# Seven block products instead of eight in the spatial product of batches 2 to 7

## Chip, core and metric

One core of one Trainium2 chip. The metric is device time in microseconds, the median of several executions; the kernel before takes 1388.6 us (1387.6 to 1389.8 in four runs). TensorE is written PE, VectorE DVE, ScalarE ACT, GpSimd POOL, SyncE SP, as in the profile.

## The reference

```python
X = np.fft.fft(np.fft.fft(x, axis=1), axis=2).real   # x: 8 x 3072 x 256
h = np.maximum(X @ w_in, 0.0)                        # d_ff = 1024
u, v = h[..., :512], h[..., 512:]
v_n = (v - mean(v)) / sqrt(var(v) + 1e-6)            # over the last axis
v_s = einsum('ts,bsd->btd', w_spatial, v_n) + b_spatial[None, :, None]
out = (u * v_s) @ w_out                              # 8 x 3072 x 256, fp32
```

The product with `w_spatial` (3072 x 3072, called W) is most of the work. `w_spatial` is drawn with a standard deviation of 0.01/3072 and the bias is 1, so the product adds some 0.01/3072 x sqrt(3072) = 0.0002 to a 1. This matters for reading the runs: the comparison with the reference hardly sees W (one experiment below uses wrong operands of W and passes). "Correct" says that nothing else was broken; that the sums are right rests on the code.

## The kernel before

The Fourier transform is done as folds on DVE followed by small cosine products on PE ("prep" of the next batch, spread over the current one in numbered steps). W is turned and cast to bf16 during batch 0 and kept in DRAM as 24 tiles of 128 x 6 x 512 (768 KB). Each batch streams them through a ring of five:

```python
def load_wt(c, g):
    wt = wtpool.tile([P, GK, TC], BF16, name="wt", tag="wt")       # ring of 5
    nc.sync.dma_start(out=wt, in_=wtd[c][g])
    return wt

def spatial(v, wt, pw, g, dt):                # 4 PSUM banks, one for each dt
    for kk in range(GK):
        k = GK * g + kk
        nc.tensor.matmul(pw, lhsT=v[:, k, 128 * dt:128 * dt + 128], rhs=wt[:, kk, :],
                         start=(k == 0), stop=(k == KT - 1))

def gate(c, pw, ut):
    gt = gpool.tile([P, TC], BF16, name="gt", tag="gt")
    tm = tpool.tile([P, TC], FP32, name="tm", tag="tm")
    nc.vector.tensor_tensor(out=tm, in0=pw, in1=bbc[:, TC * c:TC * c + TC], op=ALU.add)
    nc.vector.scalar_tensor_tensor(out=gt, in0=ut, scalar=0.0, in1=tm, op0=ALU.max, op1=ALU.mult)
    return gt
# ... (cut)
# one step of the main loop: 6 matmuls, then whatever prep is due at this step
for dt in range(NDT):
    spatial(cur.v, wts[ti], pws[dt], g, dt)
    if g == NG - 1:
        gts.append(gate(c, pws[dt], uts.pop((c, dt))))
    # ... (cut: turning of W, projection, u)
    for f in steps[4 * (NG * ci + g) + dt]:
        f()                                  # folds, transforms, v of the next batch
```

## Time and profile before

| | us |
|---|---|
| median time | 1388.6 |
| start until the first spatial product | 71 |
| batch 0 (with the turning of W) | 212 |
| batches 1 to 6, each | 158.4 |
| batch 7 (no prep beside it) | 151 |

The lengths are worked out from the trace: from the first weight load of a batch's spatial product to that of the next. The lines of the profile are shown in the prediction below.

### The profile page before, as it was taken

The page shows a single profiled execution, that of the slowest core. Times are in us where ns is not written, and L with a number is a line of the kernel's source. Part 1 is how long each engine was busy: PE and PEld are TensorE (multiplying, and loading weights), DVE is VectorE, ACT ScalarE, POOL GpSimd, SP SyncE. Part 2 cuts the span into 40 slices and gives each one's busy share as a digit, 9 for nine tenths or more (in the row PEclk, how much of TensorE's full clock was granted, in tenths as well). Part 3 has the DMA queues.
Part 4 walks back from the last instruction along what each step waited for, and adds up shares of the span by engine and source line. Part 5 has one row for each costly group of instructions (what it writes and reads, how often), then busy time and mean ns, then how long its engine had stood idle before and what let it go on. Part 6 is the DMA issues. An engine that isn't in the chain of part 4 may idle for free.

```text
span 1384.1 us, 18120 instructions
## 1 busy us (share of the span) xinstructions
PE 1321.3 (95%) x6967; PEld 651.3 (47%) x6967; DVE 842.1 (61%) x1694; ACT 516.9 (37%) x890; POOL 128.6 (9%) x167
## 2 busy tenths in 40 slices
PE   1768999999999999999999999999999999999998
PEld 0434455544444444444444444444444444444444
DVE  7656657775567747675557746776466746762323
ACT  7863146521444134531444224530445214441110
POOL 8355134410000000000000000000000000000000
PEclk9989999999999999999999999999999999999999
DMA  7899699785444543356344653456344553444441
GB/s 241 290 361 336 201 296 301 277 313 176 156 134 150 197 171 130 137 185 226 107 137 150 201 168 130 132 182 227 107 139 148 178 185 111 136 154 160 150 147 54
DMA packets 105254, 255.28 MB, mean 184 GB/s; under 512 B 17584, under 2 KB 64336, under 8 KB 105168
## 3 DMA queue, kind: packets, MB, share of 16 engines
q1 hardware_dynamic: 65840, 196.66, 42.3%
q10 hardware_dynamic: 29824, 44.05, 8.8%
q0 software_dynamic: 9504, 13.42, 3.1%
q8 instruction: 54, 0.88, 0.3%
q14 instruction: 32, 0.26, 0.1%
HBM read 210.80 MB, written 56.62 MB: 193 GB/s over the span
## 4 chain that ended last, share of the span: by engine, by line
PE 87%; DMA 5%; DVE 3%; ACT 2%; POOL 2%; issue 1%; ACTq 0%; SPq 0%; POOLq 0%; DVEq 0%
PE pw L624 68%; PE po L640 6%; DMA wr<-in_moe_w_spatial_dram 3%; PE pu L602 3%; PE pv L526 2%; PE pe L461 1%; PE pud L604 1%; PE pd L553 1%; PE pt L204 1%; DVE tm L630 1%; DMA xr<-in_x_dram 1%; DVE gt L631 1%; DMA wtd<-wx 1%; POOL xr L129 1%; POOL wb L191 0%
## 5 line engine op out<-in xcount | busy, mean ns | idle before, releaser
L624 PE MATMUL pw<-wt,v_t 128*128 128x512 bf16 x4512 | 1025.2, 380 | 7.8 <-ACT v_t L588 6.3
L624 PEld LDWEIGHTS <-v_t 128*128 128x128 bf16 x4608 | 446.4, 98 | 528.0 <-issue 10.8
L644 ACT COPY ot<-po 128x512 f32<-128x512 f32 x96 | 56.3, 586 | 403.6 <-PE po L640 392.2
L630 DVE TENSOR_TENSOR tm<-pw,bbc 128x512 f32<-128x512 f32 x192 | 131.5, 685 | 100.4 <-PE pw L624 90.3
L588 ACT ACTIVATE v_t<-r,rs 128x512 bf16<-128x512 f32 x96 | 78.4, 817 | 89.0 <-DVE rs L586 82.7
L640 PE MATMUL po<-wob,gt 128*128 128x256 bf16 x768 | 99.7, 273 | 1.7 <-DVE gt L631 1.7
L607 ACT ACTIVATE up<-pu 128x512 bf16<-128x512 f32 x96 | 57.3, 597 | 113.0 <-PE pu L602 73.6
L191 POOL CAST wb<-wr 128x768 bf16<-128x768 f32 x87 | 77.2, 893 | 134.8 <-PE pt L204 91.3
L640 PEld LDWEIGHTS <-gt 128*128 128x128 bf16 x768 | 74.7, 98 | 29.8 <-DVE gt L631 2.2
L574 DVE BATCH_NORM_STATS2 stt<-r 128x6 f32<-128x512 f32 x108 | 72.5, 680 | 23.6 <-ACT r L567 22.0
L204 PE MATMUL pt<-ident,wb 128*128 128x128 bf16 x576 | 48.9, 228 | 29.8 <-POOL ident L275 21.7
L580 ACT ACTIVATE rs<-mv,epst 128x2 f32<-128x2 f32 x96 | 28.5, 297 | 124.3 <-DVE mv L576 115.0
L631 DVE SCALAR_TENSOR_TENSOR gt<-up,tm 128x512 bf16<-128x512 bf16 x96 | 69.2, 720 | 3.3
L631 DVE SCALAR_TENSOR_TENSOR gt<-um,tm 128x512 bf16<-128x512 bf16 x96 | 67.2, 700 | 3.3
L204 PEld LDWEIGHTS <-wb 128*128 128x128 bf16 x576 | 41.0, 102 | 50.4 <-ACT wb L189 24.4
L567 ACT ACTIVATE r<-r 128x512 f32<-128x512 f32 x84 | 52.8, 628 | 28.2 <-DVE r L561 26.5
L526 PE MATMUL pv<-weo,eo_t 128*128 128x512 bf16 x192 | 57.8, 382 | 3.4 <-ACT r L536 2.7
L554 ACT ACTIVATE r<-pv 128x512 f32<-128x512 f32 x84 | 49.3, 587 | 27.0 <-PE pv L526 26.7
L602 PE MATMUL pu<-eo_t,weo 128*128 128x512 bf16 x192 | 57.5, 381 | 0.0
L562 DVE BATCH_NORM_STATS2 stt<-r 128x6 f32<-128x512 f32 x84 | 57.4, 684 | 0.0
L590 DVE TENSOR_SCALAR v_t<-r,mv,rs 128x512 bf16<-128x512 f32 x96 | 52.4, 546 | 0.0
L209 ACT COPY wt<-pt 128x768 bf16<-128x768 bf16 x44 | 35.1, 797 | 33.4 <-PE pt L204 33.3
(599 smaller groups left out, 1008.3 us busy)
## 6 DMA issues: line engine op xcount, KB each, us to landing
wt<-wtd SPq DMA_DIRECT2D x168, 768.0 KB, 4.4
wr<-in_moe_w_spatial_dram SPq DMA_DIRECT2D x69, 384.0 KB, 3.7
out_dram<-ot ACTq DMA_DIRECT2D x88, 256.0 KB, 3.9
wtd<-wt ACTq DMA_DIRECT2D x20, 768.0 KB, 5.3
xr<-in_x_dram POOLq DMA_DIRECT2D x32, 384.0 KB, 13.6
xt<-in_x_dram SPq DMA_DIRECT2D x21, 512.0 KB, 4.0
xt<-xr SPq DMA_DIRECT2D x21, 512.0 KB, 5.0
wr<-in_moe_w_spatial_dram SPq DMA_DIRECT2D x23, 383.5 KB, 7.0
```

What stands on the lines that cost most here:

```text
L191: nc.gpsimd.tensor_copy(out=wbs[i], in_=src)
L204: nc.tensor.transpose(pt[:, kk, :], wb[:, 128 * kk:128 * kk + 128], ident)
L526: nc.tensor.matmul(pv, lhsT=eo[:, kt, sl], rhs=weo[:, kt, DH:], start=(kt == 0), stop=(kt == 1))
L562: nc.vector.bn_stats(out=stt[:, 0, :], in_=r[0])
L574: nc.vector.bn_stats(out=stt[:, n, :], in_=r[n])
L588: nc.scalar.activation(out=v[:, k, :], in_=r[0], func=AF.Identity, scale=rs[:, 0:1], bias=rs[:, 2:3])
L602: nc.tensor.matmul(ps, lhsT=weo[:, kt, wd], rhs=eo[:, kt, sl], start=(kt == 0), stop=(kt == 1))
L607: nc.scalar.activation(out=up, in_=ps, func=AF.Relu)
L624: nc.tensor.matmul(pw, lhsT=v[:, k, 128 * dt:128 * dt + 128], rhs=wt[:, kk, :], start=(k == 0), stop=(k == KT - 1))
L630: nc.vector.tensor_tensor(out=tm, in0=pw, in1=bbc[:, TC * c:TC * c + TC], op=ALU.add)
L631: nc.vector.scalar_tensor_tensor(out=gt, in0=ut, scalar=0.0, in1=tm, op0=ALU.max, op1=ALU.mult)
L640: nc.tensor.matmul(po[:, i, :], lhsT=gts[dt][:, t0:t0 + 128], rhs=wob[:, dt, :], start=(dt == 0), stop=(dt == NDT - 1))
```

## The change

Split W into 2 x 2 blocks of 1536 and V into 2 x 2 blocks of 1536 x 256; the product takes seven products of sums of blocks (Winograd's form of Strassen's method) instead of eight. The sums of W do not depend on the batch: they are made once, beside batch 1, from the tiles that pass through, and stored in DRAM. The sums of V are made in every batch. Intent: 72 of 576 matmuls fewer in each of six batches.

```diff
+    class Sums:                                   # beside batch 1
+        def pool(self, k):                        # 18 times, 128 x 3072 bf16
+            o, x_, y_ = {1: (y22, y21, y22), 3: (y21, x11, y21), 4: (y21, x12, y22)}[k]
+            nc.gpsimd.tensor_tensor(out=o, in0=x_, in1=y_, op=ALU.add if k == 1 else ALU.subtract)
+        def two(self, n):                         # 12 halves on DVE
+            nc.vector.tensor_tensor(out=y22[:, sl], in0=y22[:, sl], in1=x11[:, sl], op=ALU.subtract)
+        def store(self, k):
+            nc.sync.dma_start(out=std[k - 1][c][h], in_=y22 if k < 3 else y21)
 ... (cut)
+    def t_sum(v, k, h):                           # sums of V, 8 a batch, 128 x 1536 bf16
+        e = nc.gpsimd if k in (4, 1) else nc.vector
+        e.tensor_tensor(out=o, in0=x_, in1=y_, op=ALU.add if k == 2 else ALU.subtract)
 ... (cut)
+    def after(p, d, pw, bt, bb, us):              # eviction of product p
+        a0, a1, a2 = (acc(k, d) for k in range(3))
+        if p == 1:
+            nc.scalar.copy(out=a1, in_=pw)
+            nc.gpsimd.tensor_tensor(out=a2, in0=a1, in1=bt, op=ALU.add)
+        elif p == 6:
+            plus(a1, pw, a1)                      # DVE, one input in PSUM
+            nc.gpsimd.tensor_tensor(out=a0, in0=a1, in1=bt, op=ALU.add)
+            nc.gpsimd.tensor_tensor(out=a1, in0=a1, in1=bb, op=ALU.add)
+        elif p == 7:
+            plus(a1, pw, a1)
 ... (cut: products 4, 2, 5, 3 with the gates)
+            for pi, p in enumerate(ORDP):         # [1, 6, 7, 4, 2, 5, 3], for each of 3 pairs of chunks
+                pws = [psW.tile([P, TC], FP32, name="pw", tag="psW") for _ in range(2)]
+                for h in range(2):
+                    wt = fetched[at]              # ring of 5, 42 tiles a batch instead of 24
+                    for d in range(2):
+                        for j in range(GK):
+                            nc.tensor.matmul(pws[d], lhsT=station(p, cur.v, h, j, d),
+                                             rhs=wt[:, j, :], ...)
```

Besides: bias is loaded per chunk instead of once, x is loaded from ACT's queue instead of SP's, some normalisations move from DVE to ACT, and the folds are cut into six parts at steps of their own (`FOLD2`).

## The prediction

> **What bounds the kernel now.** I read the page's engine shares and slices first, then the chain that ended last, then the groups of instructions, then the windows by stage, and last the waits of TensorE and the timeline of VectorE where GpSimd works beside it.
>
> ```profile
> PE 1321.3 (95%) x6967; PEld 651.3 (47%) x6967; DVE 842.1 (61%) x1694; ACT 516.9 (37%) x890; POOL 128.6 (9%) x167
> PE   1768999999999999999999999999999999999998
> POOL 8355134410000000000000000000000000000000
> DMA  7899699785444543356344653456344553444441
> PE 87%; DMA 5%; DVE 3%; ACT 2%; POOL 2%; issue 1%; ACTq 0%; SPq 0%; POOLq 0%; DVEq 0%
> ```
>
> TensorE is busy without a gap from slice 4 on and holds 87% of the chain that ended last; the DMA is half idle there, and GpSimd has nothing to do after slice 9. The chain's lines give 68% to L624, the spatial product. By stage (columns: stretch, length, busy time of PE, PEld, DVE, ACT, POOL, clock, DMA share, GB/s):
>
> ```profile
> 80.00:100.00 20.00, 16.48 (x114) 8.79 (x113) 11.34 (x32) 11.83 (x21) 6.71 (x9) 0.89 1.03 390
> 120.00:281.00 161.00, 157.12 (x1009) 84.41 (x1008) 114.36 (x217) 70.62 (x118) 58.40 (x69) 1.00 0.80 277
> 597.00:754.00 157.00, 157.00 (x792) 75.92 (x790) 100.05 (x205) 56.59 (x101) 0.00 (x0) 1.00 0.47 159
> ```
>
> One steady batch fills TensorE wholly, VectorE to 64%, ScalarE to 36%, and moves 159 GB/s. Busy time of a pipelined matmul is not its cost, so I take the cost from the chain in order of time (start, length, what):
>
> ```profile
> 751.57 11.65 PE pw L624 x54
> 910.23 11.65 PE pw L624 x54
> ```
>
> 54 spatial matmuls take 11.65 us, 0.2158 us each. The same place of two successive batches is 158.66 us apart (910.23 - 751.57; other places give 158.4), of which 576 x 0.2158 = 124.3 us are the spatial product. The other 34 us (projection, u, v, transforms) the change leaves alone. Groups that I use below:
>
> ```profile
> L624 PE MATMUL pw<-wt,v_t 128*128 128x512 bf16 x4512 | 1025.2, 380 | 7.8 <-ACT v_t L588 6.3
> L630 DVE TENSOR_TENSOR tm<-pw,bbc 128x512 f32<-128x512 f32 x192 | 131.5, 685 | 100.4 <-PE pw L624 90.3
> L631 DVE SCALAR_TENSOR_TENSOR gt<-up,tm 128x512 bf16<-128x512 bf16 x96 | 69.2, 720 | 3.3
> L588 ACT ACTIVATE v_t<-r,rs 128x512 bf16<-128x512 f32 x96 | 78.4, 817 | 89.0 <-DVE rs L586 82.7
> L590 DVE TENSOR_SCALAR v_t<-r,mv,rs 128x512 bf16<-128x512 f32 x96 | 52.4, 546 | 0.0
> ```
>
> L624 waited 7.8 us in the whole run: nothing but the count of matmuls can shorten the steady stages.
>
> **What the Trainium skill says.** (1) "VectorE: DVE Perf Modes", the section on the TRN2 errata, gives 215 ns for a 512-wide matmul and 691 ns for a 512-wide fp32 add; the trace has 215.8 and 685, so both costs are at their floor. (2) "GPSIMD Engine Reference", section 3.1, puts a two-input elementwise operation at about 2.6 cycles an element at 1.2 GHz. The trace has one such warm operation, 128x258 in 696 ns (L332), against 559 by the rule, so about 0.14 us of start more. Estimates from it: 512 wide 1.25 us, 1536 wide 3.5, 3072 wide 6.8. (3) "SBUF — State Buffer", "Who interferes with whom": a VectorE instruction with two SBUF inputs, or in a 2-port mode, contends with GpSimd. The trace agrees; the first line is beside GpSimd's casts, the second without them:
>
> ```profile
> 126.00 0.68 DVE L361 COPY ef<-sm 128x8 f32<-128x8 f32 x1
> 144.98 0.17 DVE L361 COPY ef<-sm 128x8 f32<-128x8 f32 x1
> ```
>
> (4) "HBM Reference", "Specifications (TRN2)": a core streaming alone gets about 425 GB/s. The best 20 us here moved 390.
>
> **The change, part by part.** *Removed:* for batches 2 to 7 the 2x2 block product takes 7 products instead of 8. Each is 3 chunks x 2 x 2 x 6 = 72 matmuls, so 504 stand for 576: 72 x 0.2158 = 15.54 us a batch, all on the path, and six batches give **-93.2 us**.
>
> *VectorE, a steady batch:* for each of three pairs of chunks there are now 14 adds from PSUM and 8 gate multiplies where there were 8 and 8, so 42 + 24 a batch stand for 24 + 24: 18 x 0.685 = +12.3. Four sums of V (1536 wide; at the fold's fp32 rate of 1.23 us for 1024 at most 1.8 each): +7. Moved to ScalarE: 12 normalisations x 0.546 = -6.6 and four evictions of the transform (L508, 1.07) = -4.3. Net about +8: 108 of 143 us, 76% instead of 64%. ScalarE gets 6 copies (0.59), 12 normalisations (0.82), 4 evictions (1.12, as L463): +18, so 74 of 143. GpSimd gets 18 adds of 1.25 and 4 sums of 3.5: 36.5 us. None reaches 143, so by busy time all of it lies beside TensorE. What matters is lateness: a product has two PSUM banks of four, and its banks must be evicted within the next product, 24 matmuls or 5.2 us, plus what else stands in between. With VectorE at 76% and in order, some products will be late. I choose 1.7 us a batch: **+10**.
>
> *DMA, a steady batch:* 42 operand tiles of 0.786 MB for 24, plus 1.6 MB of bias: 25.0 MB (159 GB/s x 157 us) become 40.7, or 285 GB/s over 143 us. Today 159 GB/s cost a share of 0.47, so the new share is about 0.84. Hidden, if the ring of five tiles evens out the bursts.
>
> *Batch 1:* GpSimd forms 18 sums of 3072: 18 x 6.8 = 122 us of 158, in a tight order: a ring slot is freed only when the sums using it have been stored. Each of the three rounds has GpSimd operations back to back, four steps (6.6 us) apart, exactly their estimated length; beside them VectorE has about 56 us of instructions that share its port (3 folds x 6.9, 24 gates x 0.7, 12 normalisations x 0.55, 12 half sums near 1). Slack before a tile comes late I work out as 5 us a round: 46 us at the fifth sum's planned end, 4.4 for a store, 4.4 for the load, against the use at 59. I take 3 us lost a round: **+9**. At the seam to batch 2 the last sums, their stores and five loads follow each other with no work beside: **+4**.
>
> *Start:* the 1.5 MB bias load leaves the stretch where the DMA share is above 1: **-1** (up to 4).
>
> Sum: 1389.5 - 93.2 + 10 + 9 + 4 - 1 = **1318 us**, 5.1% faster.
>
> **The rivals.** *Loads become the bound.* In the first chunk of a batch fall 14 tiles (11.0 MB), three x loads (3.15), the turning of x (1.6), the outputs of two chunks (1.05) and bias (0.5): 17.3 MB in 42 us (168 x 0.2158 + u 2.6 + projection 3.5), 409 GB/s. Four tiles in hand make it (17.3 - 3.1) / 42 = 338. The 390 GB/s of the start speaks against a stall, the 277 at share 0.80 and the x bursts on another queue for one. If 300 GB/s is all there is, 5 us a batch are lost: about 1335 to 1345.
>
> *VectorE and GpSimd block each other.* If GpSimd's 36 us hold VectorE for half of that, VectorE is at 88% and the products wait 5 us a batch: some 1338. The stretched copy above speaks for it; against it, that most added adds read PSUM and one SBUF input.
>
> *Batch 1 is bound by GpSimd.* If 122 us and the 56 us of VectorE exclude each other, the batch takes 178 us or more instead of 158: +20 to +40 in place of my +9, 1330 to 1350.
>
> **Range and chances.** All waits gone gives 1389.5 - 93.2 - 4 = 1292, below the range since tight orders seldom run free. One rival in full gives about 1345, the upper end. Only two or three in full bring less than 2% (above 1362). So 1299 to 1345, faster 0.92, same 0.06, slower 0.02.
>
> **What would show it.** Right: the page after has 432 fewer spatial matmuls; batches 3 to 6 lie 143 to 146 us apart; TensorE's waits there are on VectorE's adds and sum to under 3 us a batch; batch 1 lasts 160 to 170 us; DMA share near 0.84. Wrong: a distance above 148 with waits on the operand tile (loads) or on the adds (VectorE); GpSimd's 3072-wide sum far from 6.8 us; batch 1 above 175; a first batch that is longer because its chunks wait for bias.

## More of the kernel before

A batch has three folds. Each reads one x tile of 1 MB (`xt`, a single buffer) and loads the next only when it is done with it. A fold is fourteen short DVE instructions, of which twelve read two SBUF tensors and two copy a few elements.

## The result

1425.1 us (1422.7 to 1425.5), against 1388.6: ratio 1.026 (95% interval 1.024 to 1.028), 2.6% slower. A ratio here is the mean time of one kernel's runs over that of the other's of the same rounds, so not quite the ratio of the medians quoted. Executions over 1.5% slower than the fastest of the same kernel are left out of the means. The page after: engine shares, slices and the chain by engine.

```profile
PE 1267.4 (89%) x6535; PEld 619.2 (44%) x6535; DVE 1022.5 (72%) x1759; ACT 588.3 (41%) x1006; POOL 452.2 (32%) x317
```

```profile
PE   1779999978879777999879989999799989999998
POOL 8354134162454552221420250123220152025210
PEclk9989999988989898999999999999999999999999
DMA  7799689725737397779767897689767877778985
```

```profile
PE 67%; DVE 18%; DMA 9%; issue 3%; ACT 2%; POOL 1%; ACTq 0%; SPq 0%; DVEq 0%; POOLq 0%
```

The 432 matmuls are gone (6967 - 6535). But PE now has gaps from slice 8 on where it had none, DVE has 18% of the chain instead of 3%, and the granted clock dips after the start too (mean 0.959; 0.995 before). By batch:

| us | start | b0 | b1 | b2 | b3 | b4 | b5 | b6 | b7 |
|---|---|---|---|---|---|---|---|---|---|
| before | 70.8 | 211.6 | 158.4 | 158.4 | 158.4 | 158.7 | 158.4 | 158.4 | 151.0 |
| after | 71.4 | 212.5 | 217.7 | 162.3 | 158.6 | 152.3 | 158.4 | 153.3 | 136.7 |

By arithmetic batches 2 to 6 should take 158.4 - 15.5 = 142.9. So 59 us were lost in batch 1, 70 in batches 2 to 6 (784.9 against 5 x 142.9 = 714.5), and about 1 us in each of the others. The stage view, for batch 1 before, then for batches 1 and 3 after (stretch, length, busy time of PE, PEld, DVE, ACT, POOL, clock, DMA share, GB/s):

```profile
283.00:441.50 158.50, 158.50 (x798) 76.60 (x797) 101.33 (x207) 56.72 (x102) 1.43 (x2) 1.00 0.52 178
283.80:501.50 217.70, 174.29 (x797) 80.09 (x796) 178.32 (x215) 56.37 (x102) 103.89 (x17) 0.89 0.51 188
663.90:822.50 158.60, 147.02 (x726) 70.71 (x725) 118.61 (x213) 70.19 (x124) 38.98 (x26) 0.97 0.78 269
```

In batch 1 DVE is busy for 178 us with about as many instructions as it did in 101 us before. The timelines say why. First GpSimd's, then DVE's, then PE's, in batch 1 (start, length, what, and in brackets the idle time before it and its releaser):

```profile
303.88 6.85 POOL L912 TENSOR_TENSOR wt<-zone,wt 128x3072 bf16<-128x3072 bf16 x1
310.69 5.98 POOL L912 TENSOR_TENSOR wt<-wt 128x3072 bf16<-128x3072 bf16 x1
316.74 6.30 POOL L912 TENSOR_TENSOR wt<-zone,wt 128x3072 bf16<-128x3072 bf16 x1
```

```profile
304.91 5.85 DVE L399 COPY ef<-sm 128x8 f32<-128x8 f32 x1
310.79 6.42 DVE L401 TENSOR_TENSOR ef<-sm 128x508 f32<-128x508 f32 x1
317.24 6.08 DVE L408 TENSOR_TENSOR od<-ef 128x258 bf16<-128x258 f32 x1
323.25 0.41 DVE L409 TENSOR_TENSOR evf<-ef 128x258 f32<-128x258 f32 x1
```

```profile
306.88 2.75 PE L678 MATMUL pw<-wt,v_t 128*128 128x512 bf16 x12
324.85 7.69 PE L678 MATMUL pw<-zone,v_t 128*128 128x512 bf16 x24 [15.22 <-DVE tm L694]
```

A copy of eight elements, 0.17 us undisturbed, takes 5.85. DVE and GpSimd alternate: each GpSimd sum holds one DVE instruction for its whole length, and as soon as that has run the next sum holds the next one. DVE works in order, so the gate (`tm`, L694) behind the fold starts at 324.11, though the first matmuls that it evicts had ended at about 305, and PE waits 15.2 us for the PSUM banks. An instruction that reads PSUM and one SBUF tensor (L694) kept its 0.68 us throughout (0.66 to 0.72 in all 192). PE's waits for these gates in batch 1:

```profile
PE pw L678 <- DVE tm L694: 36.4, 8, 15.2
```

The idle PE then loses its clock. "TensorE: Matmul & The Clock Gate", Part 1, says that it falls to half after an idle window of about 3.4 us; the trace agrees: the clock records of batch 1 hold 48 us at half clock, in multiples of 3.4 us, and before there were none after the start. At a mean of 0.89 this is at most 24 of the 59 us, part of it while PE idled anyway; PE's waits in batch 1 sum to 43 us, which leaves about 16 for it.

In a steady batch both kinds of trouble appear, here at batch 3 (DVE with one line of GpSimd, PE, then ACT's queue):

```profile
687.70 3.18 DVE L431 TENSOR_TENSOR he<-ovf 128x128 bf16<-128x128 f32 x1
690.80 3.04 DVE L433 COPY ho<-od 128x2 bf16<-128x2 bf16 x1
687.59 6.23 POOL L934 TENSOR_TENSOR v_t<-v_t 128x1536 bf16<-128x1536 bf16 x2
719.08 1.23 DVE L395 TENSOR_TENSOR sm<-xt 128x1024 f32<-128x1024 f32 x1 [8.52 <-DMA bt<-in_moe_b_spatial_dram]
```

```profile
694.49 4.44 PE L1092 MATMUL pw<-wt,v_t 128*128 128x512 bf16 x12 [3.94 <-DVE zone L946]
721.56 2.72 PE L1092 MATMUL pw<-wt,v_t 128*128 128x512 bf16 x6 [7.04 <-DVE zone L946]
```

```profile
704.11 0.53 ACTq L165 DMA_DIRECT2D xt<-xr  x1
```

At 687 to 694 GpSimd's two sums of V (6.2 us together) hold two tiny fold instructions, and PE loses 3.9 us. At 710 to 719 DVE idles for 8.5 us: the next fold (`sm`, L395) needs x, whose load was issued at 704 and lands 15 us later (the view names the bias load because it landed last by the profile; `sm` reads only x). Evictions that were ready stand behind it, PE loses 7.0 us and comes back at half clock (six matmuls in 2.72 us instead of 1.46). The same x load made DVE wait 8.5, 2.2, 8.4 and 3.2 us in batches 3 to 6, and these took 158.6, 152.3, 158.4 and 153.3 us: the long waits and the long batches go together. A wait for x is not harmful in itself: the kernel before has one of 4.1 us in each batch, and PE lost nothing by it.

So there are two theories for two stages. *Port theory*: GpSimd's long two-input instructions hold DVE's instructions with two SBUF inputs, and its copies within SBUF, for their whole length. *Load theory*: x comes late, at the head of DVE's in-order queue. Rivals: the DMA of the sums or GpSimd's total work sets batch 1; operand tiles or the 512-wide bias additions on GpSimd set the steady batches.

### The profile page after: what moved, and what is told of

Read it like the earlier page. It is cut to its first block, busy times and chain, and to the rows that moved or that the text cites. A ratio compares the mean times of both kernels' runs of the same rounds, so it can differ in the third digit from the quotient of the medians.

```text
span 1423.2 us, 18037 instructions
## 1 busy us (share of the span) xinstructions
PE 1267.4 (89%) x6535; PEld 619.2 (44%) x6535; DVE 1022.5 (72%) x1759; ACT 588.3 (41%) x1006; POOL 452.2 (32%) x317
## 4 chain that ended last, share of the span: by engine, by line
PE 67%; DVE 18%; DMA 9%; issue 3%; ACT 2%; POOL 1%; ACTq 0%; SPq 0%; DVEq 0%; POOLq 0%
PE pw L1092 40%; PE pw L678 9%; PE po L711 5%; DVE um L698 3%; DMA xt<-xr 3%; DMA zone<-in_moe_w_spatial_dram 3%; PE pv L570 2%; PE pu L653 2%; DVE tm L694 2%; DVE v_t L641 2%; DVE up L698 2%; DMA bt<-in_moe_b_spatial_dram 1%; PE pe L506 1%; PE pt L236 1%; PE pd L597 1%
## 5 line engine op out<-in xcount | busy, mean ns | idle before, releaser
L1092 PE MATMUL pw<-wt,v_t 128*128 128x512 bf16 x1728 | 406.7, 389 | 38.2 <-DVE zone L946 31.5
L1092 PE MATMUL pw<-wt,zone 128*128 128x512 bf16 x1296 | 298.7, 379 | 0.0
L1092 PEld LDWEIGHTS <-v_t 128*128 128x128 bf16 x1728 | 171.7, 100 | 246.2 <-issue 58.3
L953 POOL TENSOR_TENSOR zone<-zone,bt 128x512 f32<-128x512 f32 x36 | 47.5, 1320 | 597.2 <-ACT zone L952 585.6
L678 PE MATMUL pw<-wt,v_t 128*128 128x512 bf16 x768 | 187.0, 386 | 10.6 <-DVE tm L694 5.0
L678 PEld LDWEIGHTS <-v_t 128*128 128x128 bf16 x1152 | 114.2, 101 | 183.7 <-issue 65.3
L1092 PEld LDWEIGHTS <-zone 128*128 128x128 bf16 x1296 | 125.8, 98 | 143.5
L694 DVE TENSOR_TENSOR tm<-pw,zone 128x512 f32<-128x512 f32 x144 | 97.5, 677 | 41.1 <-PE pw L1092 34.9
L223 POOL CAST zone<-zone 128x768 bf16<-128x768 f32 x87 | 75.5, 872 | 137.9 <-PE pt L236 92.4
L678 PE MATMUL pw<-zone,v_t 128*128 128x512 bf16 x288 | 74.9, 417 | 31.6 <-DVE tm L694 31.6
L698 DVE SCALAR_TENSOR_TENSOR um<-um,tm 128x512 bf16<-128x512 bf16 x96 | 90.4, 942 | 2.1
L698 DVE SCALAR_TENSOR_TENSOR up<-up,tm 128x512 bf16<-128x512 bf16 x96 | 83.5, 870 | 3.3
L956 POOL TENSOR_TENSOR zone<-zone,bt 128x512 f32<-128x512 f32 x36 | 48.1, 1336 | 53.9 <-DVE zone L946 52.1
```

Source lines behind the costliest of these rows:

```text
L223: nc.gpsimd.tensor_copy(out=wbs[i], in_=src)
L694: nc.vector.tensor_tensor(out=tm, in0=pw, in1=a, op=ALU.add)
L698: nc.vector.scalar_tensor_tensor(out=ut, in0=ut, scalar=0.0, in1=tm, op0=ALU.max, op1=ALU.mult)
L1092: nc.tensor.matmul(pws[d], lhsT=station(p, cur.v, h, j, d), rhs=wt[:, j, :], start=(h == 0 and j == 0), stop=(h == 1 and j == GK - 1))
```

## The experiments

All ratios are against the kernel before, run in the same rounds; where no interval is given it is within 0.6% of the ratio either way. The batch lengths (b1, b2, mean of b3 to b6) are from each kernel's profiled run, a single execution. That of t_dve was the fastest of its four (1390.6 us), those of x_sched (1327.7) and turn_late (1329.8) were slower than the median by 9 us, so a steady batch can be off by about 2 us.

| kernel | us | ratio | b1 | b2 | b3 to b6 |
|---|---|---|---|---|---|
| changed kernel | 1425.1 | 1.026 | 217.7 | 162.3 | 155.7 |
| w_split | 1393.1 | 1.004 | 176.5 | 166.3 | 157.6 |
| w_dve | 1371.7 | 0.990 | 164.7 | 156.7 | 156.1 |
| t_dve | 1398.6 | 1.008 | 218.5 | 160.2 | 147.4 |
| all_dve | 1346.0 | 0.970 | 164.7 | 157.9 | 149.9 |
| x_none (wrong) | 1302.7 | 0.938 | 161.3 | 146.7 | 142.9 |
| x_sched | 1318.5 | 0.951 | 165.7 | 158.0 | 144.6 |
| bias_dve | 1353.6 | 0.976 | 171.7 | 160.5 | 150.1 |
| bias_x | 1346.7 | 0.971 | 172.9 | 152.6 | 148.8 |
| x_none_gp (wrong) | 1399.8 | 1.008 | 217.0 | 162.2 | 149.6 |
| turn_late | 1320.8 | 0.949 | 164.2 | 158.6 | 146.2 |
| fold_late | 1358.0 | 0.978 | 166.1 | 155.4 | 154.0 |
| dma_half (wrong) | 1321.1 | 0.951 | 165.8 | 152.8 | 144.7 |

### The port: w_split, w_dve, t_dve, all_dve

*w_split*: the same sums, cut into six.

```diff
-            nc.gpsimd.tensor_tensor(out=o, in0=x_, in1=y_, op=...)
+            for j in range(GK):
+                nc.gpsimd.tensor_tensor(out=o[:, j], in0=x_[:, j], in1=y_[:, j], op=...)
```

> Batch 1's sums of W stay on GpSimd but each 3072-wide instruction is cut into six of 512; result correct. Port theory (a two-input GpSimd instruction keeps a two-SBUF-input VectorE instruction waiting for its whole length, and VectorE works in order): GpSimd's work stays near 110 us in batch 1, but no VectorE instruction is held longer than about 1.3 us, so batch 1 falls from 220 us to 165 to 185 and the kernel to 1370 to 1390. Rivals: if the stores and loads of the sums, or GpSimd's total work, set batch 1, cutting changes nothing: 215 to 225 us, kernel 1420 to 1430.

*w_dve*: the sums of W on DVE.

```diff
-            nc.gpsimd.tensor_tensor(out=o, in0=x_, in1=y_, op=...)
+            nc.vector.tensor_tensor(out=o, in0=x_, in1=y_, op=...)
```

> Batch 1's eighteen 3072-wide sums move from GpSimd to VectorE; result correct. Port theory: VectorE's own instructions are no longer stretched (180 us busy in batch 1 goes back to about 116, plus 18 sums of some 1.8 us = 32), batch 1 takes 160 to 180 us, kernel 1365 to 1385. Rival (DMA of the sums, ring slots freed late): batch 1 stays above 205 us. Rival (VectorE overloaded by its own work): above 190 us with VectorE busy over 95% of it.

*t_dve*: the sums of V on DVE.

```diff
-        e = nc.gpsimd if k in (4, 1) else nc.vector
+        e = nc.vector
```

> Only the two sums of V that the changed kernel has on GpSimd (four instructions of 1536 a batch) move to VectorE; result correct. Port theory: batches 2 to 6 lose the stretched VectorE instructions beside them and most of the TensorE waits, 157 us falls to 147 to 151 each, kernel 1385 to 1405, batch 1 unchanged at 220. Rival (late x loads or operand tiles by DMA congestion set the steady batches): they stay within 2 us of 157, kernel 1415 to 1430.

*all_dve*: both.

> Both moves together: all sums of W and of V on VectorE, GpSimd keeps only the 512-wide additions of bias; result correct. Port theory: the two gains add up, about 50 from batch 1 and 30 from the steady batches: 1330 to 1350 us, faster than both kernels. If they do not add up (the second only uncovers the late x loads), 1360 to 1375.

Batch 1 in the stage view, w_split and then w_dve; the eight-element copy in w_split; a sum of W on DVE, in all_dve (busy us, mean ns):

```profile
283.70:460.20 176.50, 164.45 (x798) 77.88 (x797) 143.64 (x220) 57.07 (x102) 136.78 (x101) 0.96 0.60 223
```

```profile
285.30:450.00 164.70, 160.80 (x798) 77.14 (x797) 136.21 (x235) 56.24 (x102) 0.00 (x0) 0.99 0.67 244
```

```profile
301.07 1.00 DVE L399 COPY ef<-sm 128x8 f32<-128x8 f32 x1
```

```profile
L912 DVE TENSOR_TENSOR wt<-zone,wt 128x3072 bf16<-128x3072 bf16 x12 | 21.0, 1747 | 0.0
```

Cutting alone takes 41 us off batch 1, although GpSimd now works longer (137 us instead of 104). It was therefore neither GpSimd's total work nor the stores, but the length of the single hold: the eight-element copy takes 1.00 us beside the 512-wide pieces, where it took 5.85. Moving the sums takes 53 us off with the same DMA traffic at a higher rate (244 GB/s instead of 188), which rules out the DMA. It is also cheap: a sum that GpSimd does in 6.1 us takes DVE 1.75. Both lengths of batch 1 and w_dve's time lie in the ranges of the port theory; w_split's time is 3 us above its range, and its batches 2 to 6 are together 12 us longer than the changed kernel's, for which no cause was sought.

t_dve leaves batch 1 alone and brings batches 3 to 6 from 155.7 to 147.4, inside the expected 147 to 151 (by the median run it would be about 149, an estimate that puts its 8 us on these four). In all_dve the gains add within 1 us (53.4 + 26.5 = 79.9 by the medians; 79.1 measured; so close an agreement is partly chance, as t_dve's runs spread over 18 us), and the kernel beats both.

### What is left: x_none, x_sched, bias_dve, bias_x

all_dve's steady batches still take 149.9 us instead of 142.9.

*x_none*: from batch 3 on x is not loaded again.

```diff
-            xin[b, a] = load_x(b, a, xrs[b])
+            if b < 3:
+                xin[-1] = load_x(b, a, xrs[b])
+            xin[b, a] = xin[-1]
```

> On top of all_dve (1346 us): from batch 3 on, x is not loaded again, the fold works on what the tile holds; result wrong on purpose. In all_dve VectorE, in order, waited 28 us in four steady batches for the x load at the head of its queue. If those waits are what is left of the steady loss (batches 3 to 6 at 150 us against 142.9 by arithmetic), they fall to 143 to 145 us and the kernel to 1318 to 1325. Rival (GpSimd's 512-wide bias additions holding VectorE's folds): stays at 148 or more, kernel above 1337.

*x_sched*: more steps between an x load and its use.

```diff
-FOLD2 = [(2, 3, 4, 5, 6, 7), (12, 12, 13, 14, 15, 16), (22, 23, 24, 25, 25, 26)]
+FOLD2 = [(1, 2, 2, 3, 4, 5), (13, 13, 13, 14, 14, 15), (24, 24, 24, 25, 25, 26)]
```

> On top of all_dve: the three folds of a batch are spread so that 8 and 9 steps instead of 5 and 6 lie between the issue of an x load and its first use; result correct. If the late x load is what is left, most of x_none's gain comes: 1322 to 1335. Rival (bias additions): within 4 us of 1346.

*bias_dve*: bias added from PSUM on DVE.

```diff
         if p == 1:
-            nc.scalar.copy(out=a1, in_=pw)
-            nc.gpsimd.tensor_tensor(out=a2, in0=a1, in1=bt, op=ALU.add)
+            plus(a2, pw, bt)
+            plus(a1, pw, bb)
         elif p == 6:
             plus(a1, pw, a1)
-            nc.gpsimd.tensor_tensor(out=a0, in0=a1, in1=bt, op=ALU.add)
-            nc.gpsimd.tensor_tensor(out=a1, in0=a1, in1=bb, op=ALU.add)
+            plus(a0, pw, a2)
 ... (and bt, bb of the next pair of chunks are loaded at step 8 of this one)
```

> On top of all_dve: no addition on GpSimd at all in batches 2 to 7 (bias is added from PSUM on VectorE, 24 more VectorE additions in place of 18 on GpSimd and 6 copies on ScalarE, net 18 x 0.69 = 12 us more VectorE work a batch), and bias is loaded 20 steps earlier; result correct. If port contention by the 512-wide additions is what is left: 1325 to 1338. Rival (late x loads): no gain, 1340 to 1352, or slower from VectorE's extra work.

*bias_x*: both.

> bias_dve and x_sched together; result correct. If both causes are real, the gains add: 1312 to 1325, batches 3 to 6 at 144 to 146. If VectorE is now too full (some 122 of 143 us), no better than the better of the two alone.

A steady batch of x_none, then of x_sched, in the stage view:

```profile
735.60:878.50 142.90, 142.14 (x711) 69.57 (x724) 110.70 (x217) 70.60 (x124) 26.80 (x22) 1.00 0.83 276
```

```profile
754.80:898.70 143.90, 142.26 (x711) 69.64 (x724) 108.86 (x217) 69.97 (x124) 27.33 (x22) 1.00 0.86 296
```

Without the x loads the four batches take 142.9 us each, the arithmetic to a tenth, with the operand tiles still moving at 276 GB/s and GpSimd's bias additions still there. Neither operand tiles nor bias additions cost anything there; in batches 3 to 6 the late x was all that was left. The kernel came out 15 us below the expected range mainly because batch 2 gained 11 us too (146.7). x_none also takes the loads' own traffic away; x_sched keeps it (296 GB/s) and gets most of the gain in a correct kernel: 1318.5 us, 5% faster than before (interval 0.948 to 0.955).

bias_dve agrees from the other side: GpSimd had nothing left to do in the steady batches, and they stayed at 150.1; DVE still waited 33 us for x in batches 3 to 6. As DVE also got more work (busy 115.8 us in batch 3, 110.8 in all_dve), x_none is the cleaner test. bias_x did not add as hoped: x arrived late in spite of the wider steps (26 us of DVE waits, 5 in x_sched), and batch 1 of both kernels is 7 to 8 us longer than in all_dve, with 10 us of DVE waits for x there (1.9 in all_dve). For batch 1 the traces offer a cause that no run tests: with no additions in its queue, GpSimd issued the last twelve pieces of the turning of x at 265 to 298 us (586 to 887 in all_dve), and the longest of these waits ends at 311. Why x stays later than in x_sched in the steady batches was not settled; bias is also loaded earlier there.

### Why x is late, and how much of the loss it was: x_none_gp, dma_half

*x_none_gp*: x_none's edit on the changed kernel itself.

> The changed kernel as it is, GpSimd sums and all, but x is not loaded again from batch 3 on; result wrong on purpose. It parts the steady loss (batches 2 to 6 at 157 us against 142.9) between the two causes. If they are independent and add, it gains what x_none gained over all_dve, 43 us: 1380 to 1385, batches 3 to 6 at 149 to 151. If GpSimd's sums of V alone are enough to stall (the x load hidden behind them), less than half of that: above 1400.

It parts the steady loss. Batches 3 to 6 take 155.7 us as changed, 149.6 without x loads (-6.1), 147.4 with the sums of V off GpSimd (-8.3) and 142.9 with both (-12.8): two causes that nearly add. The time, 1399.8, missed the stated 1380 to 1385 and just escaped the rival's "above 1400": batch 2, which x_none improves by 11 us, stayed at 162.2 here, and the other four gained 24 us instead of 28.

*dma_half*: all_dve with every second operand tile used twice.

```diff
-            wt = ring()
-            nc.sync.dma_start(out=wt, in_=operand(*stream[len(fetched)]))
+            if len(fetched) % 2:
+                wt = fetched[-1]
+            else:
+                wt = ring()
+                nc.sync.dma_start(out=wt, in_=operand(*stream[len(fetched)]))
```

> all_dve (1346 us) with its x loads as they are, but only every second operand tile is fetched from batch 2 on and used twice; result wrong on purpose. Is the x load late because the operand tiles fill the DMA? Then x lands in 4 to 6 us instead of some 9, and batches 3 to 6 go from 150 us to 143 to 145, kernel 1315 to 1325 (batch 2 too gains its 12 us: down to 1305). Rival (x is late because ScalarE's queue issues it late, behind its own work and VectorE's): 148 or more, kernel above 1338.

The DMA issues of the second half of an x load (KB each, median us to landing) in the kernel before, in all_dve and in dma_half:

```profile
xt<-xr SPq DMA_DIRECT2D x21, 512.0 KB, 5.0
```

```profile
xt<-xr ACTq DMA_DIRECT2D x18, 512.0 KB, 10.0
```

```profile
xt<-xr ACTq DMA_DIRECT2D x18, 512.0 KB, 4.8
```

These medians are weak: the profile gives a landing for only 1, 3 and 4 of the 21, 18 and 18 loads. Where the fold stood waiting for x, its start tells the landing too. So read, the second x load of batches 3 to 6 took 5.0 to 5.1 us from issue in the kernel before, 8.6 to 15.0 in the changed kernel, 10.1 to 14.6 in all_dve and 8.0 to 9.4 in dma_half. DVE's waits for x (us, times, longest), all_dve in batches 3 to 6 and dma_half in batches 2 to 6:

```profile
DVE sm L395 <- DMA xt<-xr: 28.3, 8, 8.2
```

```profile
DVE sm L395 <- DMA xt<-xr: 11.8, 5, 2.9
```

In batches 3 to 6 alone dma_half's waits are 9.1 us, and the steady batches fall to 144.7, as expected, with the loads issued from the same queue at the same steps. So x is late mostly because the operand tiles fill the DMA, not because ACT's queue issues it late. Not wholly: with half the tiles the second load still takes 3 to 4 us more than before. The change also moved the x loads from SP's queue to ACT's, and no run moves them back. Batch 2 gained only 5 of the 12 us hoped for.

### Better still? turn_late, fold_late

*turn_late*: on x_sched, the turning of x a half batch earlier.

```diff
-        if b + 2 < B:
-            xrs[b + 2] = turn_x(b + 2)
+        if b + 3 < B:
+            steps[40].append(lambda b=b: xrs.update({b + 3: turn_x(b + 3)}))
 ... (and turn_x(4) at step 60 of batch 1)
```

> On top of x_sched (1318 us): the turning of x in DRAM (1.6 MB read and written) moves from the start of a batch, where the DMA ran at 400 to 413 GB/s for 27 us, to the middle of the batch before; result correct. If the x load is late because the first chunk asks for more than the DMA gives, this takes load away there: batch 2 falls from 158 us to 146 to 152, kernel 1304 to 1314. If it is late for another reason (order of issue on ScalarE's queue), within 4 us of 1318.

1320.8 us, but in two groups (1311.6, 1311.9, 1329.8, 1333.7). The last run counts as slow; the profiled one is 1329.8, with batch 3 at 154. The interval of the other three, 0.942 to 0.956, holds x_sched's ratio: inconclusive. Batch 2, expected at 146 to 152, stayed at 158.6, so the turning is not what makes x late there.

*fold_late*: on turn_late, later folds.

```diff
-..., (13, 13, 13, 14, 14, 15), (24, 24, 24, 25, 25, 26)]
+..., (16, 16, 16, 17, 17, 17), (25, 25, 25, 25, 26, 26)]
```

> turn_late, with the second fold three steps later (11 steps after its x load) and behind the gates and u differences of its product, so that a late x holds nothing that TensorE needs soon; result correct. 1300 to 1310, batches 2 to 6 at 143 to 146. If VectorE then evicts late because the folds bunch at the third fold (25 to 26): batches 3 to 6 at 146 or more and no gain over turn_late.

A miss: 1358.0. The hold moved instead of going away: in batches 3 to 6 PE waited four times, 24.5 us in all, for the third fold (`ev`) in front of the cosine products, which stay at step 29:

```profile
PE pe L506 <- DVE ev L410: 24.5, 4, 7.9
```

## Why the prediction was wrong

**The steps that held.** The 15.54 us a batch that the missing matmuls are worth: x_none's batches are 142.9, which is 158.4 - 15.5. GpSimd's instruction lengths: 6.8, 3.5 and 1.25 us estimated, 6.1, 3.1 and 1.3 measured. The DMA share in steady batches, about 0.84 foreseen: 0.76 to 0.82, and 0.86 where PE no longer stalled (x_sched). The ring of five did even out the operand tiles: none of PE's waits in batches 3 to 6 is put down to one.

**The step that failed first: "I take 3 us lost a round: +9".** Batch 1 lost 59 us. The port was in the text, and the contention rival named this batch, but the step reckoned it as time added to GpSimd, 5 us of slack a round against lengths that nearly fit. What the runs showed is the other direction: each of 18 instructions can hold a DVE instruction for its full 6 us, the two engines alternate, and behind the held one stand the evictions that PE needs. The slack (5 us in the text; its own figures, 59 - 46 - 4.4 - 4.4, give 4.2) was for a late tile, and no such slack takes three holds in a row (18 us at 305 to 323). The rival's +20 to +40 had the exclusion right and the bound wrong: GpSimd was busy for only 104 of the 218 us, and w_split made it busier and the batch shorter. It also left out the half clock that follows a long idle stretch. "Batch 1 above 175" was one of the prediction's own signs of being wrong.

**The second: "I choose 1.7 us a batch: +10".** Batches 2 to 6 lost 14 us each on average (70 in all). The term counted DVE's busy time, 76%, and called the rest lateness. In batches 3 to 6 two single waits made nearly all of it: the sums of V on GpSimd (6 to 8 us a batch) and the x load at the head of DVE's queue (6 to 7). The V sums were put down as 3.5 us beside other work, without asking what DVE has next to them. The rival "VectorE and GpSimd block each other" named this wait and put 5 us a batch on it; its counter-argument, that most added adds read PSUM, held for the adds (0.68 us) but not for the folds and gate multiplies in the same queue (the latter rose from about 0.7 to 0.9 us on average). Of batch 2's 19 us, x_none leaves 4, near the +4 for the seam, which no run tests alone; the -1 for the start did not come (1.4 us longer by the end of batch 0).

**The rival "loads become the bound" was half right.** Its 409 GB/s in the first chunk was a fair sum, and the DMA was nearly full there (a share of 0.90 to 0.97 in the first 32 us of batch 3). But it looked for the loss at the operand tiles, which have five buffers; the transfer with one buffer and an in-order engine waiting for it was x. Its landing time rose from 5 us to between 8.6 and 15.0 (second load of a batch, changed kernel), and no buffer covered that; a second buffer for x was not tried.

**The chances.** "Only two or three in full bring less than 2%": they came together. That one brings the other is not shown: the two steady causes nearly add. But they act through the same in-order queue of DVE, and the long stalls of PE were followed by half clock. The low chance of slower, 0.02, rested on taking every added instruction as hidden if its engine had room.

## What to carry to other kernels

Room on an engine is not enough: ask how long one instruction can hold a shared port, and what stands behind the held one in an in-order queue. A long two-input GpSimd instruction beside two-input DVE work was here better moved to DVE (3.5 times faster) or cut short. When a change multiplies one stream's traffic, look at the landing time of every other load, and first at those with a single buffer.

## What the Trainium skill lacked or had wrong

- "SBUF — State Buffer": "Who interferes with whom" says of two-input instructions only that they contend with GpSimd's reads. That the side that comes second is blocked for the whole instruction, two SBUF inputs included, stands on the same page under "SBUF: two separate sides", and the trace agrees: 0.43 us became 6.08 beside a 6.3 us sum. So the skill had the fact, and the prediction's sum did not use it. What the page lacks is the remedy: six pieces instead of one took 41 us off a 218 us stage.
- "GPSIMD Engine Reference", section 3.1, compares GpSimd and DVE in fp32 alone: DVE is 1.96 times as fast for a two-input operation. With bf16 operands in SBUF the factor here was 3.5 (6.1 against 1.75 us for 3072 elements).
- No page puts the chain together that cost most here: a port hold, an in-order DVE, late PSUM evictions, an idle PE, half clock. "TensorE: Matmul & The Clock Gate" tells it for waits on DMA and on PSUM; its 3.4 us window fits the trace (48 us at half clock in batch 1, in multiples of 3.4).
- No page puts a number on how the landing time of a small load grows with other queues' traffic, before the DMA is full on average: the second 512 KB of an x load took 5.0 us at a share of 0.47 and 10.1 to 14.6 at 0.82 to 0.83 (all_dve), counted from issue to the fold that waited for it.
